# Attention and two gated layers on one core: the first loads in another order

## The chip, the core and the metric

One core of a Trainium2 chip runs the whole program in one launch. The metric is the device time of the program in microseconds. It was run three times: the median is 1088.05 us (1087.73 to 1089.42).

## What is computed

Decayed causal attention over 4 batches x 8 heads, 576 positions, 64 dimensions, then two gated layers (512 to 1536 to 512) over the 2304 tokens. Cut to what matters:

```python
log_f = np.log(np.clip(f, 0.0001, 1.0))
cum = np.cumsum(log_f, axis=-1)
scores = scale * q @ k.T + (cum[..., :, None] - cum[..., None, :])   # causal
attn = softmax(scores)
x = (attn @ v) as (2304, 512)
x = x / rms(x) * rms_g
x = (silu(x @ w_gate) * (x @ w_val)) @ w_out      # layer 1
x = (silu(x @ w_gate2) * (x @ w_val2)) @ w_out2   # layer 2
```

The weights arrive as 64-bit floats, the rest as 32-bit floats.

## The kernel before

**Tiles and stages.** The tokens are worked in four groups (`GROUPS`), each of which takes two batches: group 0 is the first 256 positions of batches 0 and 1, group 1 the same of batches 2 and 3, groups 2 and 3 the remaining positions. For each group attention makes the tile that the two layers then read; attention of the next group lies between the matrix products of the current one (`moe`, lines 1702 to 1704: three products per weight piece, since operands are split into a high and a low part). The weights come in 72 pieces, each 128 x 512; a piece of 512 KB is loaded as 64-bit data, turned into 32-bit floats by bit operations (`convert`, lines 1621 to 1663), stored, and split into high and low (lines 303 to 308).

**The first stage.** The decays `f` (32 rows: batch and head) are loaded first (line 327), clipped (line 501), put through a logarithm and summed along the row by a scan (line 506, `decay`). The sums enter the scores as two extra rows of the product: a key/query tile `qk` has 64 rows of data and two rows (`D`, `D + 1`) that hold the sums of the keys or queries and, elsewhere, constants from `aug` (line 405). In group 0, batch 0, the rows of all four pairs of heads are written by two small transfers (`decay_rows`, line 532), which need the scan; a later pair has its own two (line 571). A score product of the first stage (lines 660 and 661, `pair_queries`) needs the pair's key/query tile (line 563, `pair_kq`, 256 KB for two heads) and these rows; the values (line 591, `pair_v`, 192 KB) come in at line 736. After the scores: a maximum (line 674), exponentials (line 682), a sum and its reciprocal (688, 689), a scaling (702, 704), transposes (721), and the product with the values (736). There are four key/query buffers and three value buffers in this stage, so a fifth load waits until a scored head frees its buffer.

**What sets the order.** All instructions are written out at build time by a planner (`Plan.run`). Every piece of work is a thread that yields requests with an estimated duration and the events that it depends on. Over and over the planner takes the request that can start earliest, and among those within 0.01 us the one with the lowest priority number, and appends it to its engine's queue. The engines then run their queues in order, each waiting for what the data need. SP issues all transfers, in one queue. Its loads of pairs have priority 2.8 and up (`A_PRIO` less 0.2), the stores of the sums for later use (`keep`, line 538) 2.9, the first eight weights 4.5 (`W_EARLY`), and the rows of line 532 0.02. While the planner sees PE without work early on, it fills about half the gap with products on zeros (`fill`, line 374), after 22 products ahead of everything (line 383).

**The gates.** `cum_here` is the event of the first scan. A key/query load of head number i (counted over the group's first 16 heads, even ones only) waits for it if `i >= 2 * SP_GATE` and a value load if `i >= 2 * SP_GATE - 2` (lines 1527 and 1528); weight number `W_FREE` waits for it at line 1622, and each weight is taken up after the one ahead of it. With the values of before (`SP_GATE` 3, `W_FREE` 1) three key/query tiles and two value tiles are not gated, nor is weight 0.

Of the kernel before, what the change touches and what calls it, by code (L numbers as in the profile page):

```python
# [83 lines left out]
MB = 2  # L84
W_PRIO = 2
A_PRIO = (3, 4, 4.1, 4.1, 2.5, 4.2, 4.2, 0.5)
W_FREE = 1
A16, D16, S16 = 0.65, 0.447, 0.447
W_EARLY, W_FIRST = 4.5, 8
SPLIT_M = 0  # L90
HAND_LO = (0.3, 0.6, 1.43, 0.8, 0.3)
WARM, PE_START = 22, 6.9
SP_START, SP_GATE = 1.55, 3
FILL_GAP = 0.1
FILL = 0.5
FILL_STEP = 12
# [177 lines left out]
def tile_attention_moe_moe(  # L274
# [219 lines left out]
    def later(ev, src):  # L494
        ev.t = src.t
# [1125 lines left out]
    def convert(i):  # L1621
        x, e0 = yield Take(w64_slots, (w_raw[i - 1],) * (i > 0) + (cum_here,) * (i == W_FREE))
        later(w_raw[i], e0)
# [325 lines left out]
```

## Time and profile before

| what | value |
|---|---|
| median of three runs | 1088.05 us (1087.73 to 1089.42) |
| the profiled execution | 1089.15 us |
| its span, first to last instruction | 1087.4 us |
| mean granted clock of TensorE | 0.993 |
| PE busy | 1074.0 us, 99% of the span |
| VectorE (DVE), ScalarE (ACT), GpSimd (POOL) busy | 793.0, 618.6, 460.7 us |

The profile is of one execution; times in its rows count from the start of the span. PE is TensorE's product instructions and PEld its weight loads; SPq is SP's queue, whose rows show how long issuing took, not the transfer. "Idle before" is the time for which an engine stood still ahead of a group of instructions, with what released it. Ends of products are modelled, so a row's length is a little more than the distance to the next one's start. The granted clock is a share of 2.4 GHz: 1.00 is that and 0.50 is 1.2 GHz.

### The profile page before, as it was taken

Reading aid. Unit: us, or ns where it says so; the run is one execution under the profiler, and the core shown is the slowest. Engines: PE = TensorE matmul, PEld = TensorE weight load, DVE = VectorE, ACT = ScalarE, POOL = GpSimd, SP = SyncE. Lnnn points to the kernel's source line nnn. Section 1 sums busy time; section 2 is a strip of 40 time slices with the busy share of each in tenths; the row PEclk is TensorE's granted clock in tenths of the full one; section 3 lists DMA queues with packets and bytes.
Section 4 is the critical chain, followed back from the end, with each engine's and each line's share of the span. In section 5 each row is a group of like instructions: output and inputs, shape, how many; then the busy total and the mean of one; then the engine's idle time right before and its main releaser. Section 6 shows DMA issues by size and latency. Waiting matters only on the chain.

```text
span 1087.4 us, 17697 instructions
## 1 busy us (share of the span) xinstructions
PE 1074.0 (99%) x5542; PEld 947.7 (87%) x5542; DVE 793.0 (73%) x1695; ACT 618.6 (57%) x1428; POOL 460.7 (42%) x487
## 2 busy tenths in 40 slices
PE   8999999999999999999999999999999999999998
PEld 7978888888888888888888888888889999999998
DVE  5988878988456646777657776777777878788773
ACT  4976778976456645667425665456643334543352
POOL 0213201234266766666525684557732440243310
PEclk8999999999999999999999999999999999999999
DMA  7755889875897775776799899997895557755583
GB/s 211 232 187 174 269 268 338 275 240 192 304 384 270 250 261 194 273 248 230 255 352 362 314 359 387 362 317 269 299 351 202 191 181 240 241 173 168 200 257 105
DMA packets 136498, 282.23 MB, mean 260 GB/s; under 512 B 14674, under 2 KB 57490, under 8 KB 136402
## 3 DMA queue, kind: packets, MB, share of 16 engines
q1 hardware_dynamic: 136404, 281.10, 75.2%
q8 instruction: 44, 0.72, 0.3%
q14 instruction: 50, 0.41, 0.1%
HBM read 194.32 MB, written 86.65 MB: 258 GB/s over the span
## 4 chain that ended last, share of the span: by engine, by line
PE 92%; DMA 3%; DVE 2%; ACT 1%; POOL 1%; issue 1%; SPq 0%; ACTq 0%; POOLq 0%
PE bank L1702 18%; PE bank L1703 17%; PE bank L1704 17%; PE bank L1416 5%; PE bank L1418 5%; PE bank L1417 5%; PE bank L941 3%; PE bank L913 3%; PE bank L1326 3%; PE bank L1325 3%; PE bank L1324 3%; PE bank L804 2%; PE bank L805 2%; PE bank L660 2%; PE bank L736 2%; DMA w<-w_f 1%
## 5 line engine op out<-in xcount | busy, mean ns | idle before, releaser
L308 POOL TENSOR_TENSOR whl<-w,whl 128x512 fp32r<-128x512 f32 x126 | 167.1, 1329 | 241.2 <-ACT whl L303 204.2
L1702 PE MATMUL bank<-X,whl 128*128 128x512 f32 x564 | 226.8, 402 | 0.0
L1704 PE MATMUL bank<-X,whl 128*128 128x512 f32 x564 | 220.6, 391 | 0.0
L1703 PE MATMUL bank<-X,whl 128*128 128x512 f32 x564 | 220.3, 391 | 0.0
L303 ACT CAST whl<-w 128x512 fp32r<-128x512 f32 x178 | 108.8, 616 | 51.1 <-PE bank L1703 13.9
L1704 PEld LDWEIGHTS bank<-X,whl 128*128 128x128 f32 x564 | 106.0, 188 | 23.0
L1702 PEld LDWEIGHTS bank<-X,whl 128*128 128x128 f32 x564 | 106.3, 188 | 20.2
L1703 PEld LDWEIGHTS bank<-X,whl 128*128 128x128 f32 x564 | 106.3, 188 | 19.0
L1702 PE MATMUL bank<-H,whl 128*128 128x512 f32 x215 | 87.0, 405 | 0.0
L1704 PE MATMUL bank<-H,whl 128*128 128x512 f32 x215 | 85.1, 396 | 0.0
L1703 PE MATMUL bank<-H,whl 128*128 128x512 f32 x215 | 85.1, 396 | 0.0
L1844 ACT ACTIVATE tmp<-bank 128x384 f32<-128x384 f32 x48 | 23.6, 492 | 91.4 <-DVE bank L1454 90.7
L1834 ACT ACTIVATE tmp<-bank 128x512 f32<-128x512 f32 x72 | 43.0, 597 | 38.5 <-PE bank L1704 37.8
L308 DVE TENSOR_TENSOR whl<-w,whl 128x512 fp32r<-128x512 f32 x71 | 49.1, 699 | 19.3 <-ACT whl L303 18.3
L1836 DVE SCALAR_TENSOR_TENSOR tmp<-tmp,bank 128x512 f32<-128x512 f32 x72 | 49.2, 683 | 18.2 <-ACT tmp L1834 16.5
L1857 DVE SCALAR_TENSOR_TENSOR bank<-tmp,bank 128x512 f32<-128x512 f32 x60 | 41.6, 694 | 28.3 <-PE bank L1704 27.9
L925 DVE TENSOR_TENSOR pl<-bank,ph 128x512 fp32r<-128x512 f32 (+1 forms) x80 | 49.9, 632 | 14.4 <-ACT ph L303 13.7
L822 DVE TENSOR_REDUCE tm<-bank 128x1 f32<-128x512 f32 (+1 forms) x96 | 50.3, 560 | 11.5 <-PE bank L805 7.8
L308 POOL TENSOR_TENSOR kb<-raw,k 64x576 fp32r<-64x576 f32 x32 | 45.7, 1429 | 21.0 <-ACT k L303 18.8
L1645 ACT ACTIVATE wk<-w,kbias 128x512 uint16<-128x512 uint16 x59 | 51.3, 885 | 2.3 <-DMA w<-w 1.9
L1417 PE MATMUL bank<-X,whl 128*128 128x384 f32 x154 | 51.5, 335 | 0.0
L1418 PE MATMUL bank<-X,whl 128*128 128x384 f32 x154 | 51.5, 335 | 0.0
(297 smaller groups left out, 2840.5 us busy)
## 6 DMA issues: line engine op xcount, KB each, us to landing
whl<-w_split SPq DMA_DIRECT2D x90, 512.0 KB
w<-w SPq DMA_DIRECT2D x72, 512.0 KB
w<-w_f SPq DMA_DIRECT2D x144, 256.0 KB
w_split<-whl SPq DMA_DIRECT2D x72, 512.0 KB
w_f<-w SPq DMA_DIRECT2D x72, 256.0 KB
w_sums<-w SPq DMA_DIRECT2D x48, 256.0 KB
w_sums_split<-whl SPq DMA_DIRECT2D x23, 512.0 KB
w<-w_sums SPq DMA_DIRECT2D x41, 256.0 KB
```

The source lines that it names most:

```text
L303: nc.scalar.copy(o, i)
L308: (nc.vector if e == "DVE" else nc.gpsimd).tensor_tensor(o, a, b, op=ALU.subtract)
L822: em = yield op("DVE", dve(m), lambda: nc.vector.tensor_reduce(st[:, c + i : c + i + 1], bank[:, :m], axis=AX.X, op=ALU.max), e)
L925: e = yield op("DVE", dve(n), lambda: nc.vector.tensor_tensor(low, src, o.bitcast(F32), op=ALU.subtract), e)
L1416: nc.tensor.matmul(o, w[:, 0, cs], xh, start=c == 0, stop=False)
L1417: nc.tensor.matmul(o, w[:, 0, cs], xl, start=False, stop=False)
L1418: nc.tensor.matmul(o, w[:, 1, cs], xh, start=False, stop=c == 1)
L1645: lambda e: nc.scalar.activation(k16[:, :, 0], x16[:, :, 1], AF.Identity, scale=1.0 / 8192, bias=kbias)
L1702: nc.tensor.matmul(o, wh[:, cs], xh, start=start, stop=False)
L1703: nc.tensor.matmul(o, wh[:, cs], xl, start=False, stop=False)
L1704: nc.tensor.matmul(o, wl[:, cs], xh, start=False, stop=stop)
L1836: "DVE", dve(n), lambda: nc.vector.scalar_tensor_tensor(a, a, 1.0, b, op0=ALU.add, op1=ALU.mult), e,
```

## The change

Two constants. `SP_GATE` goes from 3 to 2: two key/query tiles and one value tile are not gated, and the third key/query tile and the second value tile now wait for the scan in the planner's order. `W_FREE` goes from 1 to 0: weight 0 waits for it too. The planner then writes the order of the whole program anew.

```diff
-W_FREE = 1
+W_FREE = 0
 A16, D16, S16 = 0.65, 0.447, 0.447
 W_EARLY, W_FIRST = 4.5, 8
 SPLIT_M = 0
 HAND_LO = (0.3, 0.6, 1.43, 0.8, 0.3)
 WARM, PE_START = 22, 6.9
-SP_START, SP_GATE = 1.55, 3
+SP_START, SP_GATE = 1.55, 2
```

## Rows read from the trace of the kernel before

**Rows 1.** Page, head and first part: span, busy time and share
```profile
span 1087.4 us, 17697 instructions
...
PE 1074.0 (99%) x5542; PEld 947.7 (87%) x5542; DVE 793.0 (73%) x1695; ACT 618.6 (57%) x1428; POOL 460.7 (42%) x487
```

**Rows 2.** Stretches: length, busy us by engine, granted clock (PEclk), DMA share, GB/s
```profile
0.00:5.00 5.00, 1.68 (x8) 1.68 (x9) 2.49 (x9) 2.83 (x4) 1.58 (x13) 1.00 0.34 98
...
8.40:10.20 1.80, 0.03 (x1) 0.00 (x1) 0.00 (x0) 0.00 (x0) 0.00 (x0) 1.00 1.06 255
...
11.30:18.10 6.80, 6.80 (x25) 5.99 (x23) 4.36 (x17) 2.80 (x13) 0.72 (x1) 0.50 0.62 209
...
15.00:22.00 7.00, 7.00 (x32) 6.55 (x32) 5.23 (x21) 3.77 (x18) 0.07 (x1) 0.54 0.40 93
22.00:44.00 22.00, 22.00 (x158) 20.94 (x157) 18.87 (x69) 20.78 (x74) 4.62 (x4) 1.00 0.97 313
...
61.30:63.50 2.20, 0.01 (x1) 0.00 (x0) 1.19 (x7) 1.21 (x3) 1.73 (x2) 1.00 0.77 236
65.90:69.20 3.30, 3.30 (x12) 2.94 (x13) 3.30 (x12) 2.83 (x9) 0.00 (x0) 0.50 0.00 0
80.00:1087.00 1007.00, 1002.31 (x5126) 882.35 (x5124) 730.47 (x1491) 560.58 (x1243) 445.95 (x462) 1.00 0.76 264
```

**Rows 3.** Timeline of SP: start, us to issue, queue, line, operation, tiles, count
```profile
0.73 0.88 SPq L327 DMA_DIRECT2D tmp<-f  x2
...
4.42 0.47 SPq L563 DMA_DIRECT2D qk<-qk  x1
5.03 1.45 SPq L532 DMA_DIRECT2D qk<-cum  x2
6.52 0.43 SPq L591 DMA_DIRECT2D v<-v  x1
7.00 0.54 SPq L563 DMA_DIRECT2D qk<-qk  x1
...
9.00 1.08 SPq L1625 DMA_DIRECT2D w<-w  x2
...
20.20 1.36 SPq L1625 DMA_DIRECT2D w<-w  x3
```

**Rows 4.** Timeline of PE: start, us, line, operation [idle before and its releaser]
```profile
10.23 0.89 PE L660 MATMUL bank<-qk 66*128 66x128 f32 x4 [1.80 <-DMA qk<-cum]
...
12.42 1.48 PE L660 MATMUL bank<-qk 66*128 66x128 f32 x4
...
18.40 3.44 PE L374 MATMUL bank<-H 128*128 128x256 f32 x16
21.67 0.82 PE L721 MATMUL bank<-mi,d 128*128 128x128 f32 x6
22.32 0.82 PE L660 MATMUL bank<-qk 66*128 66x128 f32 x4
...
23.10 0.82 PE L660 MATMUL bank<-qk 66*128 66x128 f32 x4
...
25.76 1.20 PE L374 MATMUL bank<-H 128*128 128x256 f32 x8
...
69.28 0.40 PE L1702 MATMUL bank<-X,whl 128*128 128x512 f32 x1
```

**Rows 5.** Timeline of VectorE (DVE) and GpSimd (POOL), same columns as rows 4
```profile
3.19 0.45 DVE L501 TENSOR_SCALAR tmp<-tmp 32x256 f32<-32x256 f32 x2
...
3.89 0.68 DVE L506 TENSOR_TENSOR_SCAN cum<-tmp,tmp 32x256 f32<-32x256 f32 x1 [0.25 <-ACT tmp L502]
...
14.35 0.72 POOL L1639 TENSOR_SCALAR w<-w,rebase 128x512 f32<-128x512 f32 x1 [12.10 <-DMA w<-w]
...
16.39 0.42 DVE L1637 TENSOR_SCALAR w<-w 128x512 f32<-128x512 f32 x1
...
18.85 0.61 DVE L704 TENSOR_SCALAR d<-d,tm 128x256 f32<-128x256 f32 x2
```

## The prediction

> **What bounds the kernel now.** I read the page's first part, then a table of stretches, then the timelines of SP, PE and VectorE over the first 30 us. The page says that PE is busy for 1074.0 us of a span of 1087.4 us [rows 1]. From 80 us to the end PE works 1002.31 of 1007 us at full clock [rows 2]: whatever brings the first 80 us to an end earlier moves the end of the kernel by as much, as long as the order of the later work stays sound. So the question is what bounds the start.
>
> There the table [rows 2] shows four things. PE stands still from 8.4 to 10.2 us. From 11.3 to 18.1 us it works without a break, but at a granted clock of 0.50, which is 1.2 GHz; the mean of 0.54 from 15 to 22 us says that full clock came back only half a microsecond before 22 us. The DMA engines are full around 9 us, 0.40 busy from 15 to 22 us, and full again (0.97) from 22 to 44 us. And there is one more standstill, 61.3 to 63.5 us, followed by half clock.
>
> The first standstill ends with the decay rows: the first score product starts at 10.23 us after a wait of 1.80 us for the transfer of line 532 [rows 4]. SP issued those two transfers from 5.03 to 6.48 us [rows 3], so they took up to 3.7 us to land. In this program three key/query tiles of 256 KB, two value tiles of 192 KB, the decays (72 KB) and the constants (32 KB) were issued ahead of them, 1286 thousand bytes by the shapes in the code. By 5 us 98 GB/s x 5 us = 490 thousand had moved [rows 2]; the other 796 thousand at 255 GB/s take 3.1 us, until 8.1 us, and a value tile issued at 6.52 us and a key/query tile right behind it share the engines with the rows.
>
> **The order that the planner will write.** It takes the ready request with the earliest start, then the lowest priority number. SP's loads of pairs start from 2.8, its weights are at 4.5, the rows at 0.02. With the gates closed one pair earlier SP has two key/query tiles and one value tile to issue, then nothing until the scan of the first decays; weight 0, at present not gated but always outranked, would now go into that hole, and the new W_FREE stops it. Then come the rows, value 2, key/query 3, value 3, key/query 4, the two stores of line 538, the weights. By the planner's own costs the rows come some 0.2 us earlier and the weights some 1 us later than it thinks now; so it pads PE with one fill fewer ahead of the first scores, and tends to rank weight conversions behind attention steps.
>
> **Part 1, the rows.** The scan ends at 4.57 us [rows 5], and SP's issue at 5.03 can hardly come earlier; I take the same issue, ending at 6.48 us. Ahead of it now lie 827 thousand bytes; 337 thousand are left at 5 us and gone after 1.3 us, at 6.3 us. So the second row transfer meets idle engines. How long a small transfer takes then is bounded by the decays' own load: issued from 0.73 to 1.61 us [rows 3], the first half used at 3.19 us and the second about 0.2 us later [rows 5], at most 1.8 us after the end of the issue. That gives 8.3 us; the other bound is no gain, 10.2 us. I take the first, since the empty queue is the nearer case. PE is busy with its warm products until 8.4 us anyway, so the scores start at 8.4 instead of 10.23: **-1.8 us**, between -1.9 and 0.
>
> **Part 2, the clock.** Six heads are scored in a row, from 10.23 to 18.40 us, and then come 16 fills, until 21.67 us, when the transposes of the first pair start [rows 4]. A head takes 0.78 us at full clock (22.32 to 23.10 us), and its four score products 0.82 us there and 1.48 us at half (12.42 us) [rows 4]; a fill takes 0.215 us (3.44 for 16) against at most 0.15 (1.20 for 8) [rows 4]. With the present pattern, two heads near full clock and four at half, the six take 8.2 us from 8.4 us, and 15 fills 3.2 us: the transposes at 19.8 us, -1.9. That is the small end. With full clock throughout: six heads at 0.78, to 13.1 us, 15 fills at 0.15, to 15.3 us: -6.4, the large end. I take the case between: without the standstill the clock may still fall where it fell now, by 11.3 us, since PE then does nothing but scores, and in this trace scores alone never brought it back; only the fills did, some 3 us after they began. By then 3.6 heads would be done instead of 1.3. The 2.3 heads more at full clock save some 2.3 x 0.7 = 1.6 us: **-3.5 us** in all at the transposes, which then start near 18.2 us.
>
> The Trainium skill, "TensorE: Matmul & The Clock Gate", section "What's actually happening", has the clock follow how busy PE has recently been: idleness throttles it, sustained activity releases it. The row against it is 11.3 to 18.1 us: PE 6.80 of 6.80 us busy and still at 0.50 [rows 2]. By the page's rule the closed gap would keep the full clock; that is the second rival below.
>
> Are the transposes' operands there by 18.2 us? The scaling that they need stands on VectorE at 18.85 us, behind a maximum that waits for the sixth head [rows 5]. With that head done near 14.9 us it would end by 16.0 us. If instead the first weight's conversion stays ahead of it, as now at 16.39 us [rows 5], it ends up to 3.1 us after that conversion starts. The fills cover the first case; the second costs up to 1.1 us.
>
> **Part 3, what moves back.** A value and a key/query tile move behind the rows. SP spent 0.61 us from the start of the third key/query tile to the rows and 0.48 us on a value tile [rows 3], so weight 0 is issued 1.1 us later, at 10.1 us. The engines stand idle from 6.3 us until the next tile's bytes flow, 8.3 us at the latest: 2.0 us at most. Weight 0 landed at 14.35 us [rows 5] and would land between 15.4 and 16.4 us. The cover is that SP afterwards waits at key/query tiles whose buffer a scored head must free, so that three weights are issued only at 20.20 us, 1.8 us after the sixth head [rows 3, 4]. Those releases come earlier by what PE gains, and the 0.40 busy engines between 15 and 22 us have room for it. Bounds: 0 (all in that slack) to +2.0 us. I take **+0.5 us**, since the slack of 15 to 22 us is over 4 us of engine time.
>
> **Sum.** -3.5 + 0.5 = -3.0 us at about 22 us, handed on through the DMA-bound stretch to 44 us and the rest of the first stage, because what fills the engines there was itself held by PE's releases. The new order of conversions and fills further on I cost at nothing: the cover is that PE is the bound from 80 us on; gone, it is worth a fill or two (0.1 us each) up to a standstill as at 61.3 us. The profiled execution took 1.1 us more than the median: 1089.15 - 3.0 = 1086.15, and on the median's footing 1088.05 - 3.0 = **1085.0 us**. A measurement of this kernel can tell about 0.2%, 2.2 us, from no change.
>
> **Rivals.** *Forecast*, 0.42: as above.
>
> *The clock never falls*, 0.15. For it: the fall came 1 us after the only long gap. Against it: the stretch of scores at half clock. The transposes would start near 15.3 us; the sixth head ends at 13.1 us, so the three weights are issued at 14.9 instead of 20.20 us, 5.3 us earlier, less the 0.5: 1083.2.
>
> *The head start is absorbed*, 0.24: the stretch from 22 to 44 us is bound by bytes (313 GB/s [rows 2]), and the bytes come no earlier because engines stood idle at 6.3 us. For it: 0.97 busy. Against it: 0.40 just before. About 1088.
>
> *It does not do what it says*, 0.06: the rows' landing time is their own (many small pieces on few engines), not the queue's. PE starts as now, weights 0 to 1 us later: 1088.5.
>
> *Slower*, 0.13: VectorE stands at the first weight's conversion. It is in order; if that conversion stays ahead of the first pair's steps, it now waits, and everything on VectorE behind it, the pair's scaling among it, waits too. It decides once VectorE gets there before weight 0 lands: at 16.39 less a head start of over 1 us. Then the whole first stage runs on the weights' clock, 2.0 us later, and PE's idle time ahead of the transposes brings another spell of half clock, as after 63.5 us, where 3.3 us at 0.50 [rows 2] cost 1.65 us: 1088.05 + 3.65 = 1091.7.
>
> **How the numbers follow.** Of the forecast's 0.42 nearly all is faster by over 2.2 us (0.40), with the clock rival's 0.15 that is 0.55. Same: 0.24 + 0.06 + the rest, 0.32. Slower 0.13. The range goes from 1082 us, 1 us past the clock rival's time, to 1089.5 us, 1 us past the two cases of no change; outside it lie the slower case and the extreme of the clock rival (-6.4).
>
> **What would show it.** Right: the first score product at about 8.4 us with no wait for line 532; half clock over at or before 18.5 us; the first transposes near 18 us; three weights issued near 17 us instead of 20.20; the first 512-column product some 3 us before 69.28 us [rows 4]. Wrong: a standstill on PE between fills and transposes, VectorE idle before line 1637 for a weight, or a gain at 22 us that is gone at 69 us.

## The result, and the profile after

The changed kernel is **slower**: 1103.8 us in the median against 1088.7 for the kernel before. The ratio on record is 1.0125 (95% interval 1.0104 to 1.0146), a little less than that of the two medians. The prediction, 1085.0 us with a range to 1089.5, was wrong, and on the wrong side. The lines of the page that answer to [rows 1]:

```profile
span 1098.8 us, 17839 instructions
...
PE 1079.6 (98%) x5615; PEld 951.4 (87%) x5615; DVE 785.5 (71%) x1695; ACT 621.2 (57%) x1427; POOL 466.9 (42%) x486
```

The span is 11.4 us longer, with 73 product instructions more: they are zero products (the fills of line 374 went from 104 to 177).

The loads, however, did what was forecast, and more. The timeline of SP, beside [rows 3]:

```profile
3.26 0.49 SPq L563 DMA_DIRECT2D qk<-qk  x1
4.73 1.44 SPq L532 DMA_DIRECT2D qk<-cum  x2
6.22 0.44 SPq L591 DMA_DIRECT2D v<-v  x1
...
9.96 0.55 SPq L563 DMA_DIRECT2D qk<-qk  x1
...
12.39 0.54 SPq L563 DMA_DIRECT2D qk<-qk  x1
...
14.24 0.53 SPq L563 DMA_DIRECT2D qk<-qk  x1
...
16.03 2.69 SPq L1625 DMA_DIRECT2D w<-w  x4
```

The rows go out at 4.73 us with two key/query tiles and one value tile ahead of them. But look at the last line: the first weights are issued at **16.03 us, not 9.00**. Three more key/query tiles (9.96, 12.39, 14.24 us), each with its two row transfers, stand ahead of them. Only the first two weights are really late: the third goes out at 17.0 us, 20.20 before, and the eighth at 33.5, 35.7 before.

The timeline of PE, beside [rows 4]:

```profile
3.33 4.29 PE L383 MATMUL bank<-H 128*128 128x256 f32 x22 [3.33 <-DVE H L370]
...
7.74 0.89 PE L660 MATMUL bank<-qk 66*128 66x128 f32 x4
...
12.46 1.84 PE L374 MATMUL bank<-H 128*128 128x256 f32 x14
14.13 0.93 PE L721 MATMUL bank<-mi,d 128*128 128x128 f32 x6
...
25.00 0.88 PE L721 MATMUL bank<-mi,d 128*128 128x128 f32 x6 [2.02 <-DVE d L704]
```

The scores start at 7.74 us instead of 10.23, the six heads end at 12.46 instead of 18.40, and the first transposes start at 14.13 instead of 21.67 us: a head start of 7.5 us. The clock never fell in this stretch, as the table of stretches shows beside [rows 2] (length, busy us of PE, PEld, DVE, ACT, POOL, PEclk, DMA share, GB/s):

```profile
11.30:18.10 6.80, 6.80 (x50) 6.35 (x50) 4.63 (x21) 6.24 (x25) 0.00 (x0) 1.00 0.66 161
15.00:22.00 7.00, 7.00 (x51) 6.61 (x49) 3.34 (x13) 6.52 (x24) 0.00 (x0) 1.00 0.86 289
...
60.00:112.00 52.00, 44.56 (x228) 37.03 (x229) 42.79 (x91) 39.70 (x83) 11.96 (x8) 0.93 0.71 234
```

The first of these lines reads 1.00 where it read 0.50. The first break is here on VectorE, which stands idle for the first weight's conversion:

```profile
17.45 0.17 DVE L675 TENSOR_SCALAR tm<-tm 128x4 f32<-128x4 f32 x1
20.62 0.43 DVE L1637 TENSOR_SCALAR w<-w 128x512 f32<-128x512 f32 x1 [3.00 <-DMA w<-w]
```

PE then waits 2.02 us for the scaling that is queued behind it (the 25.00 us line above).

The loss comes later. The same table for the kernel before, 60 to 112 us:

```profile
60.00:112.00 52.00, 49.35 (x239) 41.17 (x239) 43.24 (x100) 37.90 (x87) 14.92 (x12) 0.97 0.59 189
```

In these 52 us PE was busy for 49.35 us before and for 44.56 us after. The timeline of PE in that stretch of the changed kernel shows what it does in between:

```profile
61.38 0.50 PE L1702 MATMUL bank<-X,whl 128*128 128x512 f32 x1 [1.55 <-ACT X L303]
...
85.56 3.23 PE L374 MATMUL bank<-H 128*128 128x256 f32 x25
...
92.21 0.80 PE L1704 MATMUL bank<-X,whl 128*128 128x512 f32 x1 [2.40 <-POOL whl L308]
...
99.71 3.28 PE L374 MATMUL bank<-H 128*128 128x256 f32 x26
...
105.63 0.79 PE L1704 MATMUL bank<-X,whl 128*128 128x512 f32 x1 [2.18 <-DVE whl L308]
```

The layers' first product starts at 61.38 us, 7.9 us **earlier** than the 69.28 us of [rows 4]. But then it runs out of weights: 25 fills at 85.56 us, 2.40 us of idleness until GpSimd has split a weight, 26 fills, 2.18 us until VectorE has split one. Counted over the stretch, there are 82 fills instead of 25 (10.95 us of PE instead of 3.79) and 4.8 us more of idleness, 12 us in all. The groups of three products done by 112 us are 35 instead of 52; a group takes 0.70 us (two begin at 69.28 and 69.98 us in the trace of before), so 17 groups are 11.9 us, close to the 11.4 us of the span; the attention products done by 112 us are the same in both. After 112 us both kernels run alike: PE is idle for 5.0 us there, and was for 5.1.

### The profile page after: what moved, and what is told of

The parts are those of the page before. It is cut to its first block, busy times and chain, and to the rows that moved or that the text cites. A ratio compares the mean times of both kernels' runs of the same rounds, so it can differ in the third digit from the quotient of the medians.

```text
span 1098.8 us, 17839 instructions
## 1 busy us (share of the span) xinstructions
PE 1079.6 (98%) x5615; PEld 951.4 (87%) x5615; DVE 785.5 (71%) x1695; ACT 621.2 (57%) x1427; POOL 466.9 (42%) x486
## 4 chain that ended last, share of the span: by engine, by line
PE 91%; DVE 4%; DMA 2%; ACT 2%; POOL 1%; issue 1%; SPq 0%; ACTq 0%; POOLq 0%; DVEq 0%
PE bank L1702 18%; PE bank L1704 18%; PE bank L1703 17%; PE bank L1417 5%; PE bank L1416 5%; PE bank L1418 5%; PE bank L941 3%; PE bank L913 3%; PE bank L1326 3%; PE bank L1324 3%; PE bank L1325 3%; PE bank L804 2%; PE bank L805 2%; PE bank L660 1%; PE bank L736 1%; DMA w_f<-w 1%
## 5 line engine op out<-in xcount | busy, mean ns | idle before, releaser
L308 POOL TENSOR_TENSOR whl<-w,whl 128x512 fp32r<-128x512 f32 x136 | 183.2, 1348 | 286.0 <-ACT whl L303 217.8
L1834 ACT ACTIVATE tmp<-bank 128x512 f32<-128x512 f32 x72 | 43.1, 599 | 37.3 <-PE bank L1704 35.7
L308 DVE TENSOR_TENSOR whl<-w,whl 128x512 fp32r<-128x512 f32 x61 | 42.0, 695 | 16.9 <-ACT whl L303 16.7
L1656 DVE SCALAR_TENSOR_TENSOR w<-w,wk 128x512 int32<-128x512 int32 x72 | 51.3, 720 | 2.3 <-ACT wk L1645 1.2
```

The costliest lines, as they stand in the source:

```text
L308: (nc.vector if e == "DVE" else nc.gpsimd).tensor_tensor(o, a, b, op=ALU.subtract)
L1656: lambda: nc.vector.scalar_tensor_tensor(ti, ti, 3, k, op0=ALU.logical_shift_left, op1=ALU.bitwise_or), e, et,
```

## The experiments

The oddity to explain: by 112 us the changed kernel had converted more weights than the kernel before (24 instead of 19, counting the instruction of line 1656 that ends a conversion), and yet PE lacked weights. **Theory**: the planner ranks the first eight weights at 4.5 (`W_EARLY`), behind all attention work, and all later weights at 2 (`W_PRIO`), ahead of most of it. Where the first eight come late, the ninth and later ones overtake them in the queues of the engines that convert and split them, and PE, which needs them in order, waits for a weight of low rank while later ones lie ready. They come late because the fifth to seventh key/query tiles overtook them on SP. **Rivals**: A, the early attention work itself crowds out the weights; B, the head start is absorbed; C, any new order lands badly; D, the 7 us on SP's queue are the loss by themselves, and D2, the priorities are; E, the additional fills are.

**1. The early rows alone.** The order of before, with two loads moved behind the rows in the emitted program, unknown to the planner (and the same for the key/query load of `h == 4`):

```diff
-            ev = yield op("SP", 0.02, lambda: nc.sync.dma_start(o, cums[0][:H]), e)
+            def rows():
+                nc.sync.dma_start(o, cums[0][:H])
+                if i == 1:
+                    for fn in held:
+                        fn()
+            ev = yield op("SP", 0.02, rows, e)
...
+            lambda: (held.append if hds[0].g == hds[0].s == 0 and h == 2 else lambda fn: fn())(
+                lambda: nc.sync.dma_start(vv.rearrange("p c a n -> p (c a n)"), v0[b, h // 2])
```

> Edit: the planner's order of before, but the second value tile and the third key/query tile are issued behind the rows instead of ahead of them; nothing else moves. My theory (late weights, not early rows, cost the time): the early rows are a gain by themselves; scores start near 7.8 us, the six heads run at full clock, and the kernel is 2 to 6 us faster than before. Rival A (early attention work crowds out the weights on VectorE and the DMA engines): 5 to 15 us slower than before. Rival B (the head start is absorbed before 70 us): within 2 us of before.

Ratio 1.0005 (0.9987 to 1.0023): no difference. My theory's 2 to 6 us of gain are not there, rival A is out, and rival B is right. Where the head start went is to be seen in the timelines of PE and VectorE (the helper lines moved this copy's numbers: 676 is the score product of line 660, 737 the transpose of 721, 1653 the conversion of 1637):

```profile
7.91 0.89 PE L676 MATMUL bank<-qk 66*128 66x128 f32 x4
...
12.63 2.08 PE L374 MATMUL bank<-H 128*128 128x256 f32 x16
17.65 1.51 PE L737 MATMUL bank<-mi,d 128*128 128x128 f32 x6 [2.94 <-ACT d L718]
18.96 1.49 PE L676 MATMUL bank<-qk 66*128 66x128 f32 x4
```

```profile
11.94 0.17 DVE L691 TENSOR_SCALAR tm<-tm 128x4 f32<-128x4 f32 x1
15.56 0.43 DVE L1653 TENSOR_SCALAR w<-w 128x512 f32<-128x512 f32 x1 [3.45 <-DMA w<-w]
```

The scores start at 7.91 us and the fills at 12.63, almost 6 us earlier than before. Then VectorE stands for 3.45 us at the first weight's conversion, the pair's scaling behind it, and PE for 2.94 us. The transposes start at 17.65 us, 4 us earlier than before, but the clock has now fallen: the next four score products take 1.49 us. At the layers' first product nothing of the head start is left: 69.71 us against 69.28.

**2. One constant alone.** `SP_GATE` 2, and `W_FREE` left at 1:

```diff
-SP_START, SP_GATE = 1.55, 3
+SP_START, SP_GATE = 1.55, 2
```

> Edit: SP_GATE 2 as in the change, W_FREE left at 1, so that weight 0 may go into the hole ahead of the rows. My theory: weight 0 is then issued first of all weights near 4 us, nothing starves, and the rows land later than in the change because 512 KB lie ahead of them; within 4 us of before. Rival A (a key/query tile and a value tile moved behind the rows cost it, weights or not): 8 us slower or more. Rival C (any new order lands badly, whatever it does to the weights): 5 us slower or more.

Ratio 1.0015 (0.9996 to 1.0033), as expected. Weight 0 goes into the hole ahead of the rows, and the head start is gone; SP's and PE's timelines:

```profile
3.81 0.59 SPq L1625 DMA_DIRECT2D w<-w  x1
4.59 1.45 SPq L532 DMA_DIRECT2D qk<-cum  x2
```

```profile
10.85 0.92 PE L660 MATMUL bank<-qk 66*128 66x128 f32 x4 [2.25 <-DMA qk<-qk]
```

The scores wait 2.25 us and start at 10.85 us; the line names a key/query tile, and the weight load of that product waited 2.5 us for the rows. The next four weights are issued only from 21.00 us on, later than in the change. Still, the order here is new from the first weight on, and it costs nothing that can be measured: rival C does not hold as a rule. So `SP_GATE` alone does not make the change slow, and what the change has besides it is the late first weight. `W_FREE` 0 with `SP_GATE` 3 was not run.

**3. The change, with overtaking stopped.**

```diff
         for i in range(TOTAL):
+            if i == W_FIRST:
+                yield wait(w_ready[W_FIRST - 2])
             pr = (W_EARLY if i < W_FIRST else W_PRIO) + i * 0.0001
```

> Edit: the changed kernel, and the planner takes up the ninth weight only when the seventh is ready, so that weights of the higher priority cannot overtake the first eight. SP's order of the first 16 us stays that of the change. My theory (the first eight weights, late and of low priority, are overtaken, and PE starves for them between 60 and 112 us): all of the loss comes back and some of the early rows' gain shows: 1080 to 1088 us, fewer than 40 zero products between 60 and 112 us instead of 82. Rival D (the 7 us by which the first weight is issued later are the loss by themselves): 1096 us or more. Rival C: slower than before by 5 us or more.

1080.2 us, ratio **0.9922** (0.9896 to 0.9948) to the kernel before: all of the loss is back, and 0.8% beyond. The first weights are as late on SP as in the change, so rival D is out; 60 to 112 us:

```profile
16.06 1.88 SPq L1625 DMA_DIRECT2D w<-w  x4
```

```profile
60.00:112.00 52.00, 51.99 (x254) 43.27 (x253) 44.70 (x96) 40.20 (x86) 14.04 (x13) 1.00 0.64 212
```

PE is busy for 51.99 of 52 us at full clock, with 20 fills in it. The hold also keeps back the ninth weight's load (60.9 us instead of 45.4); giving the first eight weights the rank of the later ones was not tried.

**4. Late weights without early rows.** The kernel before, weight 0 held behind the fourth key/query tile:

```diff
-        x, e0 = yield Take(w64_slots, (w_raw[i - 1],) * (i > 0) + (cum_here,) * (i == W_FREE))
+        x, e0 = yield Take(w64_slots, (w_raw[i - 1],) * (i > 0) + (cum_here,) * (i == W_FREE) + tuple(held_w) * (i == 0))
...
+            if g == s == 0:
+                held_w.append(heads[6].kq_ready)
```

> Edit: the kernel before, and weight 0 waits in the planner for the fourth key/query tile, so that the fifth to seventh tiles go ahead of it as in the changed kernel; the rows stay where they were before. My theory: as slow as the change or slower, 1098 to 1112 us, though the rows are not early. Rival A: as before, within 3 us.

1104.9 us, ratio 1.0152 (1.0123 to 1.0182): the loss of the change without its early rows. SP's first weights, and the longest of PE's waits between 56 and 115 us (line 1707 is the third product, 1704 before):

```profile
20.16 1.83 SPq L1628 DMA_DIRECT2D w<-w  x4
```

```profile
PE bank L1707 <- DVE whl L308: 7.8, 1, 7.8
```

PE stands once for 7.8 us, for the split of one weight: the eighth, counted as below.

**5. The hold on the kernel before.** The edit of experiment 3, made on before.

> Edit: the kernel before, its early loads untouched, and the planner takes up the ninth weight only when the seventh is ready. My theory (overtaking costs much where the first weights are late, little where they are early): between 1 us slower and 6 us faster than before. If the hold is worth its 1.9% in any order, whatever the first loads do: about 1070 us. Rival C (any new order lands badly): 5 us slower or more.

Ratio 0.9965 (0.9945 to 0.9985): 3.8 us faster. Overtaking costs a little in the old order as well, and the 0.8% of experiment 3 is more than the hold alone; the rest, 0.4%, can be put to the change's first loads when nothing starves behind them; no run separates the two further.

**6. The change, with weight 0 ahead of the fifth pair's tile.**

```diff
+                    if i == 8:
+                        wk += (w_sp,)
                     spawn(pair_kq(heads[h : h + 2], go[0], *early, *wk), pr - 0.2)
...
+        if i == 0:
+            w_sp.t = plan.free["SP"]
```

> Edit: the changed kernel, and the fifth pair's key/query tile waits in the planner until weight 0 has been issued, so that weights 0 and 1 go ahead of it as before; priorities as in the change. My theory (the pairs' overtaking on SP's queue starts the loss): the first weights are issued near 10 us, and the time comes back to within 5 us of before, 1083 to 1094. Rival D2 (the low priority of the first eight weights is enough by itself, where they stand in SP's queue does not matter): 1098 us or more, as the change.

Ratio 0.9974 (0.9956 to 0.9992): the loss is gone, with the priorities of the change; rival D2 is out. SP and PE:

```profile
10.04 1.08 SPq L1628 DMA_DIRECT2D w<-w  x2
```

```profile
8.38 0.82 PE L660 MATMUL bank<-qk 66*128 66x128 f32 x4
...
15.50 0.85 PE L721 MATMUL bank<-mi,d 128*128 128x128 f32 x6 [0.64 <-DVE d L704]
```

The weights are back at 10.04 us, 1.0 us later than before, which is what the prediction had expected of the change. The time is 0.26% below before, some 2.8 us: near the 3.0 us that the prediction had hoped for, though not shown to come by its terms.

**7. The change without fills.** The zero products between pieces of work are left out:

```diff
-FILL = 0.5
+FILL = 0.0
```

> Edit: the changed kernel without the planner's zero products between pieces of work (the 22 ahead of everything stay); all other work in the same order. My theory (PE waits for weights there anyway): PE stands still where the fills stood, and the time is within 4 us of the change, or longer where the clock falls. Rival E (73 fills more, standing ahead of products that were ready, are the loss): 6 to 9 us faster than the change.

1106.9 us, ratio to before 1.0159 (1.0130 to 1.0188), no better than the change. Rival E is out; PE's waits from 56 to 115 us and the stretch:

```profile
PE bank L1704 <- POOL whl L308: 4.4, 2, 3.5
PE bank L1704 <- DVE whl L308: 4.3, 1, 4.3
PE bank L721 <- ACT d L702: 3.6, 2, 2.7
PE bank L1702 <- ACT X L303: 3.3, 1, 3.3
```

```profile
60.00:112.00 52.00, 34.51 (x141) 25.97 (x140) 44.77 (x99) 39.64 (x88) 13.12 (x10) 0.90 0.65 211
```

Where the fills stood, PE now stands idle: for 17.5 of the 52 us instead of 7.4, with the clock at 0.90 on average. The fills are the planner's mark for the gap, not its cause.

All kernels in one table, ordered by time. The columns behind the ratio are read from one profiled execution each. At 0.70 us a group, the count of product groups done by 112 us gives the ratio to within 0.25%.

| kernel | ratio to before | first weight issued, us | PE busy of 52 us (60 to 112) | fills there | groups by 112 us |
|---|---|---|---|---|---|
| 3, change with hold | 0.9922 | 16.06 | 51.99 | 20 | 62 |
| 5, before with hold | 0.9965 | 9.02 | 50.24 | 12 | 54 |
| 6, change, weight 0 first | 0.9974 | 10.04 | 51.11 | 35 | 53 |
| before | 1 | 9.00 | 49.35 | 25 | 52 |
| 1, rows alone | 1.0005 | 9.77 | 49.60 | 40 | 50 |
| 2, SP_GATE alone | 1.0015 | 3.81 | 50.95 | 39 | 50 |
| the change | 1.0125 | 16.03 | 44.56 | 82 | 35 |
| 4, before, weights late | 1.0152 | 20.16 | 43.75 | 114 | 30 |
| 7, change without fills | 1.0159 | 16.43 | 34.51 | 0 | 28 |

A late first weight alone does not cost it (kernel 3), nor does overtaking where the weights are early (before, and kernel 6, where the ninth weight's split ends ahead of four of the first eight, and PE waits for none); in the change and in kernels 4 and 7 the two come together. The lateness of the first weights on SP with nothing else re-ordered was not tried.

The overtaking itself can be read from the rows of the changed kernel. PE takes the weights in order, four groups to a weight, so the first 32 groups are the first eight weights. The buffers are handed out in order too (line 1613): eight named `whl`, then three named `late_h` (lines 386 to 389), which hold the ninth to eleventh weights. Line 308 makes a weight's low part; VectorE, GpSimd and PE:

```profile
67.62 1.29 DVE L308 TENSOR_TENSOR late_h<-w,late_h 128x512 fp32r<-128x512 f32 x2
75.00 0.68 DVE L308 TENSOR_TENSOR late_h<-w,late_h 128x512 fp32r<-128x512 f32 x1
...
104.90 0.67 DVE L308 TENSOR_TENSOR whl<-w,whl 128x512 fp32r<-128x512 f32 x1
```

```profile
89.11 3.05 POOL L308 TENSOR_TENSOR whl<-w,whl 128x512 fp32r<-128x512 f32 x1 [11.64 <-ACT whl L303]
```

```profile
109.55 0.40 PE L1702 MATMUL bank<-X,late_h 128*128 128x512 f32 x1
```

The wait of 2.40 us at 92.21 us stands in the 21st group, for the sixth weight, and that of 2.18 us at 105.63 us in the 29th, for the eighth. Their low parts are made at 89.11 and 104.90 us, while those of the ninth to eleventh, which PE first needs at 109.55 us, were made from 67.62 to 75.68 us, when only four of the first eight were done. In the kernel before, the same three come later, when seven of the first eight are done, and PE waits for no weight:

```profile
86.13 1.29 DVE L308 TENSOR_TENSOR late_h<-w,late_h 128x512 fp32r<-128x512 f32 x2
88.47 0.69 DVE L308 TENSOR_TENSOR late_h<-w,late_h 128x512 fp32r<-128x512 f32 x1
```

How 7 us at the first load lead to this order stays open. It is not that the first eight were converted late: by 60 us the changed kernel had ended eight conversions and the kernel before seven. They were left behind at the split.

## Why the prediction was wrong, point by point

**Part 1, the rows**: right, and undersized. -2.5 us instead of -1.8. The engines did empty: they were 0.16 busy from 6.20 to 7.00 us. The rows landed at most 1.6 us after the issue's end (6.17 to 7.74 us), as bounded from the decays' load, and the issue came at 4.73 instead of 5.03 us. PE was also free earlier than the 8.4 us I had set: its 22 warm products took 4.29 us.

**Part 2, the clock**: the direction was right, the size half. -7.5 us at the transposes instead of -3.5. I had taken it from the old trace that scores alone let the clock fall; entered at full clock and without a gap, they held it from 7.74 to 12.46 us, and the fills and transposes behind them held it too. On this point the second rival was right, and the Trainium skill's rule ("TensorE: Matmul & The Clock Gate", "What's actually happening"), which I had weighed against the row, agrees with this stretch: 6.80 of 6.80 us busy at 1.00. The old row (6.80 of 6.80 us busy with scores at 0.50) stands beside it; no run here shows why busy PE did not bring the clock back there.

**Part 3, what moves back**: this is where it first failed. "Weight 0 is issued 1.1 us later": it was 7.0 us. I had followed the planner's choice up to the stores and stopped. As I read the planner, at that point the fifth pair's buffer is free in the planner's reckoning, because the scores come earlier and the weight's turn later; then the fifth pair's tile, at 2.8, goes ahead of the weight at 4.5, and while its rows are issued the next buffer comes free. An event that shifts by 1 us changed sides with another, and the priority numbers did the rest. Experiment 6 puts that one choice back, and the weights and the time return.

**The sum**: "The new order of conversions and fills further on I cost at nothing", with PE as the bound from 80 us on for cover. That is the step that decided. The cover is not there: between 60 and 112 us PE lives on the first weights, and with overtaking it lost 12 us. I had seen that the planner "tends to rank weight conversions behind attention steps", and put no price on it; for the cover gone I had named "a fill or two" up to a standstill as at 61.3 us, which is 2.2 us. It was 57 fills more and 4.8 us more of idleness.

**The rivals**: the slower one forecast that VectorE stands at the first weight's conversion. It does (3.00 us in the change, 3.45 us in experiment 1), and PE behind it, but that only uses up the head start: experiment 1 is that case, and comes out even. The loss of the change is another mechanism, 60 us later, which no rival of mine had. "Head start absorbed" (0.24) was right of the early rows as such in its time only: it had the bytes from 22 to 44 us absorb the start, and in experiment 1 most of it goes in the wait at the conversion and the half clock behind it.

**Signs named ahead**: a first score near 8 us, early transposes and an early first product of the layers all came true, and the time was worse. The sign that spoke was the one that I had named with a value of "near 17 us instead of 20.20" for three weights, without asking for the first two: 16.03 us was the issue of all four. Two of the signs named for "wrong" came true as well: VectorE idle before line 1637, and PE idle between fills and transposes (the 3.00 and 2.02 us above). The third, a gain gone at 69 us, did not: the gain stood at 7.9 us there and was lost behind it.

## What to carry to other kernels

In a kernel whose order a planner writes, price a changed constant by the order that comes out: follow each queue on until two requests that could change places are clear of each other, and then the next consumer down the line. Where ready times decide first and priorities second, 1 us can move a load by 7. And look for pairs of ranks that invert, such as early pieces ranked low and later pieces of the same stream ranked high: the low ones are safe only as long as they are early, and one wait that keeps the stream in order was worth more here (2% on the changed kernel, 0.35% on the old one) than the loads that were moved.

## What was not expected of the hardware

Score products, back to back, ran at a granted clock of 0.50 for the 6.8 us from 11.3 us in the kernel before, after PE had stood still for 1.8 us, and at 1.00 from 7.74 to 12.46 us in the changed one, where PE came to them without a break. But a standstill is not always followed by half clock. In the changed kernel the 2.02 us ahead of 25.00 us left the clock at 1.00, and after the 2.18 us ahead of 105.63 us a product took 0.63 us instead of 0.39; the stretch of the first, and PE after the second:

```profile
22.00:44.00 22.00, 19.41 (x139) 18.14 (x137) 21.69 (x75) 18.12 (x63) 6.91 (x7) 1.00 0.87 275
```

```profile
106.22 0.63 PE L1702 MATMUL bank<-X,whl 128*128 128x512 f32 x1
```

No run here shows what sets the two apart. And a head start of 4 us at the transposes is worth nothing (1.0005) when an in-order engine behind it has a load to wait for.
